# Pooled attention ahead of a gated feed-forward product on one core: a new order of ScalarE's and VectorE's work inside the slots

## The chip, the cores and the metric

One core of one Trainium2 chip runs the whole kernel in one launch. The metric is the device time in microseconds of one execution; of several executions the median counts.

## What is computed

The reference, cut to what matters (B = 8 batches, H = 8 heads, S = 576 rows, D = 64, all float32; 4608 tokens, model width 512, inner width 1024):

```
k_p = k.reshape(B, H, 72, 8, D).mean(axis=3)          # pooling: 72 keys a head
v_p = v.reshape(B, H, 72, 8, D).mean(axis=3)
scores = (q @ k_p.T) / sqrt(D); scores -= scores.max(-1)
attn = exp(scores); attn /= attn.sum(-1) + 1e-9
x = (attn @ v_p)  ->  4608 tokens x 512               # heads side by side
out = ((x @ w1) * (x @ w2)) @ w3 @ w_out
```

The kernel multiplies w3 and w_out once into W (1024 x 512), so the last line becomes `out = ((x @ w1) * (x @ w2)) @ W`.

## The kernel before

**Exact products from two parts.** A float32 operand is written as a hi part (rounded by ScalarE's copy into another number type) and a lo part (source minus hi, on VectorE or GpSimd), and a product is three passes on TensorE: hi-hi, hi-lo, lo-hi. So each operand that TensorE is to use needs first an instruction of ScalarE, then a subtraction that waits for it: `split` (L152 hi, L153 lo), the lo parts of W_out (L177) and of w3 in the first slots (L194), R (L451 hi, L453 lo), the probabilities PT (L486 hi, L487 lo), x (L510 hi, L511 lo), g (L546 hi, L551 lo). The weights arrive in a packed form, each value as two words: `high` (L135, ScalarE) unpacks the one word, `low` (L140, VectorE) the other, and `conv_b` (L148, VectorE; "the combine") joins them. Only `low` has read the second word of the raw cell, so a later load into that cell waits for it.

**Chunks and tiles.** The 4608 tokens go in 12 chunks of 384. A chunk has 3 token tiles of 128 where it lies in one batch, and 4 of 96 where two batches meet in it (chunks 1, 4, 7, 10). Per tile the attention goes: scores of heads 0 to 3 and of heads 4 to 7 on TensorE (L404, `s_mm`, two "passes"); `soft1` for each pass: the extreme of the scores (L420, VectorE) and exp. Five tiles (chunk 0's three and two of chunk 1) have their exps on ScalarE alone, four a pass, each with its sum read out by the accumulator (L430); the others subtract on VectorE (L422), take exp on ScalarE (L425) and sum on VectorE (L426). Then `soft2` on VectorE (L439 and L441 on the sums, L442 scales all 8 heads' exps), `soft3` (R, the 8 keys of each head that don't fit the 128-wide layout, as hi on ScalarE and lo on VectorE), transposes of the probabilities (L464) and of R (L474) on TensorE, `pt_post` (PT hi and lo), and per head pair attention times v (L499 to L502) and x's hi and lo (`av_post`). In the main loop, per chunk and block j of the inner width, `a_mm` and `b_mm` (L525), `a_post` (copy, L535), `b_post` (product g, L545, and its hi), `g_lo` (L551) and `out_mm` (L560).

**What sets the order.** The program is written out by a plan: `at(kind, k, fn)` notes a step, and the steps are emitted sorted by slot (the integer part of k), then by kind in the order L (loads), P (vector and scalar work), M (main matmuls), A (attention matmuls), then by the fraction of k, then by when they were noted. Each engine runs its own instructions in the order of emission, so a step that emits for ScalarE and VectorE puts an instruction into each queue, and a waiting instruction holds up all behind it on that engine. A fraction of k matters only among steps of one kind in one slot. Slot numbers: F0 = 4 is the first slot of the product of w3 and W_out, which takes two slots for each of 16 steps; K0 = 20 is its middle, where the attention of chunk 0 begins to be prepared; M0 = 36 is the first slot of the main loop, 24 slots a chunk. `w_block` (L164) is the vector and scalar work of one weight step in the first slots: new weights (unpack), the weights of the step before (hi and w3's transpose with its lo) and W_out's lo part of two steps before. From step 8 on `w_conv`, `w_conv2` and `w_split` (L209 to L219) do the same for w3 alone. w1 and w2 are unpacked by `w12_conv`, `w12_conv2` and `w12_split` (L221 to L237) in slots M0-6 to M0+17; their lo part is on GpSimd but for three. `plan_att` (L604) places the attention of a chunk, one chunk ahead of the main loop's use; in chunk 1 a tile begins every 3 slots from M0+3. Beside it stand the pooling sums of k (`prep_k`; three of them on VectorE, L319, the others on GpSimd), the 32 x 32 transposes of q on VectorE (`tr_q`, L276), and v's remainder, the 8 keys of v that belong to R (`prep_vr`, L380: sums on GpSimd, then a copy and two scalings on ScalarE, L381 to L384; `prep_vr2`, L392: four additions on GpSimd).

**Buffers.** Scores, transposes and x share three PSUM buffers ("att", L65), so TensorE's next attention step also waits until one of the three has been read.

Of the kernel before, what the change touches and what calls it, by code (L numbers as in the profile page):

```python
# [18 lines left out]
def kernel(  # L19
# [143 lines left out]

    def w_block(v):  # L164


# [587 lines left out]
```

## Time and profile before

| | us |
|---|---|
| median of 3 runs | 807.65 (805.84 to 809.54) |
| the profiled execution | 805.16 |
| its span | 803.4 |
| TensorE busy | 777.9 (97%) |
| VectorE busy | 431.7 (54%) |
| ScalarE busy | 288.0 (36%) |
| GpSimd busy | 196.1 (24%) |
| mean granted TensorE clock | 0.989 |

The span is the time from the first to the last recorded instruction of the profiled execution; its own time has 1.8 us around that. PE is TensorE (PEld its weight loads), DVE VectorE, ACT ScalarE, POOL GpSimd, SP the queue that issues the loads. A busy share is an average over the span; an idle engine's bracket in a timeline says how long it stood still ahead of an instruction and which instruction ended that.

### The profile page before, as it was taken

The page shows a single profiled execution, that of the slowest core. Times are in us where ns is not written, and L with a number is a line of the kernel's source. Part 1 is how long each engine was busy: PE and PEld are TensorE (multiplying, and loading weights), DVE is VectorE, ACT ScalarE, POOL GpSimd, SP SyncE. Part 2 cuts the span into 40 slices and gives each one's busy share as a digit, 9 for nine tenths or more (in the row PEclk, how much of TensorE's full clock was granted, in tenths as well). Part 3 has the DMA queues.
Part 4 walks back from the last instruction along what each step waited for, and adds up shares of the span by engine and source line. Part 5 has one row for each costly group of instructions (what it writes and reads, how often), then busy time and mean ns, then how long its engine had stood idle before and what let it go on. Part 6 is the DMA issues. An engine that isn't in the chain of part 4 may idle for free.

```text
span 803.4 us, 11625 instructions
## 1 busy us (share of the span) xinstructions
PE 777.9 (97%) x4344; PEld 722.2 (90%) x4344; DVE 431.7 (54%) x873; ACT 288.0 (36%) x727; POOL 196.1 (24%) x234
## 2 busy tenths in 40 slices
PE   7899888999999999999999999999999999999998
PEld 6677777899999999999999999999999999999997
DVE  6968989465373375374374374474454455452112
ACT  5567565332243233242242333232242332332211
POOL 2155465107007302025008102034028020000000
PEclk8999999999999999999999999999999999999999
DMA  9988960045034030062043030071143110100101
GB/s 333 267 206 217 273 145 1 1 94 123 1 72 120 27 80 1 1 143 75 1 95 109 27 67 1 17 157 44 43 85 91 53 26 1 40 1 1 40 1 39
DMA packets 106632, 62.63 MB, mean 78 GB/s; under 512 B 73680, under 2 KB 90320, under 8 KB 106576
## 3 DMA queue, kind: packets, MB, share of 16 engines
q1 hardware_dynamic: 106576, 61.89, 30.1%
q8 instruction: 34, 0.56, 0.3%
q14 instruction: 22, 0.18, 0.1%
HBM read 52.43 MB, written 9.44 MB: 77 GB/s over the span
## 4 chain that ended last, share of the span: by engine, by line
PE 85%; DVE 7%; DMA 4%; issue 2%; ACT 2%; SPq 0%; DVEq 0%
PE o L560 24%; PE a L525 24%; PE b L525 23%; PE att L404 4%; PE o L586 2%; DMA st<-in_k_dram 2%; PE att L464 2%; DVE wb L140 1%; DVE wb L148 1%; PE att L501 1%; PE att L500 1%; PE att L502 1%; PE att L499 1%; PE att L474 1%; DMA raw<-in_moe_w_out_dram 1%
## 5 line engine op out<-in xcount | busy, mean ns | idle before, releaser
L525 PE MATMUL a<-xT,hl 128*128 128x384 f32 x1152 | 223.1, 342 | 0.0
L525 PE MATMUL b<-xT,hl 128*128 128x384 f32 x1152 | 220.3, 339 | 0.4 <-DVE Wc L153 0.4
L525 PEld LDWEIGHTS a<-xT,hl 128*128 128x128 f32 x1152 | 205.0, 190 | 4.9 <-POOL hl L153 0.2
L525 PEld LDWEIGHTS b<-xT,hl 128*128 128x128 f32 x1152 | 198.7, 188 | 0.8 <-DVE Wc L153 0.8
L560 PE MATMUL o<-Wc,gh 128*128 128x512 f32 x576 | 183.6, 400 | 0.0
L560 PEld LDWEIGHTS o<-Wc,gh 128*128 128x128 f32 x576 | 105.1, 189 | 17.3
L545 DVE TENSOR_TENSOR a<-b,a 128x384 f32<-128x384 f32 x96 | 53.1, 553 | 123.5 <-PE b L525 123.5
L362 POOL TENSOR_TENSOR st<-st 72x512 f32<-72x512 f32 (+1 forms) x53 | 73.0, 1377 | 173.2 <-DMA st<-in_k_dram 161.0
L560 PE MATMUL o<-Wc,gl 128*128 128x512 f32 x288 | 114.0, 396 | 0.0
L535 ACT COPY a<-a 128x384 f32<-128x384 f32 x96 | 46.1, 480 | 179.9 <-PE a L525 160.6
L546 ACT CAST gh<-a 128x384 fp32r<-128x384 f32 x96 | 49.2, 512 | 148.4 <-DVE a L545 148.4
L551 DVE TENSOR_TENSOR gl<-a,gh 128x384 fp32r<-128x384 f32 x96 | 59.4, 619 | 35.8 <-ACT gh L546 35.4
L375 POOL TENSOR_TENSOR vbd<-vm,vbd 64x256 fp32r<-64x256 f32 x16 | 13.3, 833 | 249.8 <-ACT vbd L374 248.2
L560 PEld LDWEIGHTS o<-Wc,gl 128*128 128x128 f32 x288 | 54.1, 188 | 12.5
L511 DVE TENSOR_TENSOR xT<-att,xT 128x384 fp32r<-128x384 f32 x48 | 26.5, 556 | 70.0 <-ACT xT L510 70.0
L426 DVE TENSOR_REDUCE sm<-E 128x4 f32<-128x288 f32 (+1 forms) x70 | 31.6, 451 | 46.3 <-ACT E L425 46.3
L404 PE MATMUL att<-kbd,qT 128*128 128x144 f32 (+1 forms) x320 | 52.1, 286 | 0.2 <-ACT E L430 0.2
L420 DVE TENSOR_REDUCE mx<-att 128x4 f32<-128x288 f32 (+1 forms) x80 | 36.0, 450 | 28.8 <-PE att L404 28.7
L425 ACT ACTIVATE E<-E 128x288 f32<-128x288 f32 (+1 forms) x70 | 31.1, 445 | 55.4 <-DVE E L422 55.4
L404 PEld LDWEIGHTS att<-kbd,qT 128*128 128x128 f32 (+1 forms) x320 | 46.6, 179 | 1.1 <-ACT E L430 0.5
L586 PE MATMUL o<-hl 128*128 128x512 f32 x144 | 42.3, 430 | 3.3 <-DVE hl L177 3.3
L363 POOL TENSOR_TENSOR st<-st 72x256 f32<-72x256 f32 (+1 forms) x53 | 41.8, 789 | 4.2
(87 smaller groups left out, 806.4 us busy)
## 6 DMA issues: line engine op xcount, KB each, us to landing
raw<-in_moe_w_dram SPq DMA_DIRECT2D x32, 512.0 KB
st<-in_k_dram SPq DMA_DIRECT2D x32, 288.0 KB
out_dram<-ob SPq DMA_DIRECT2D x35, 256.0 KB
st<-in_v_dram SPq DMA_DIRECT2D x32, 256.0 KB
qs<-in_q_dram SPq DMA_DIRECT2D x128, 48.0 KB
raw<-in_moe_w_out_dram SPq DMA_DIRECT2D x8, 512.0 KB
st<-in_v_dram SPq DMA_DIRECT2D x64, 64.0 KB
qs<-in_q_dram SPq DMA_DIRECT2D x96, 24.0 KB
```

The source lines that it names most:

```text
L362: nc.gpsimd.tensor_tensor(out=t[:, :, 0:4], in0=t[:, :, 0:4], in1=t[:, :, 4:8], op=ALU.add)
L363: nc.gpsimd.tensor_tensor(out=t[:, :, 0:2], in0=t[:, :, 0:2], in1=t[:, :, 2:4], op=ALU.add)
L404: nc.tensor.matmul(out=ps[:nt, 2 * KP * j:2 * KP * (j + 1)], lhsT=qT[n][:, pr, off:off + nt], rhs=kbd[b % 2][:, pr], start=True, stop=True,)
L420: nc.vector.tensor_reduce(out=mx[:nt, hs], in_=sv, axis=AX.X, op=ALU.min)
L426: nc.vector.reduce_sum(out=sm[:nt, hs], in_=E[:nt, hs], axis=AX.X)
L525: nc.tensor.matmul(out=o, lhsT=w12[j, w][sw][:, kt * P:(kt + 1) * P], rhs=x[sx][:, kt], start=(i == 0), stop=(i == 3 * NK - 1))
L535: nc.scalar.copy(out=a, in_=gt[m, j][:, :CH])
L545: nc.vector.tensor_tensor(out=g, in0=ps[:, :CH], in1=g, op=ALU.mult)
L546: nc.scalar.copy(out=gh, in_=g)
L551: nc.vector.tensor_tensor(out=gl, in0=g, in1=f(gh), op=ALU.subtract)
L560: nc.tensor.matmul(out=oacc[m][t], lhsT=(gh, gl)[sg][:, c], rhs=W[j][sw], start=(j == 0 and i == 0), stop=(j == NJ - 1 and i == 2))
L586: nc.tensor.matmul(out=wacc[h][it], lhsT=w3t[s][sa][:, it * P:(it + 1) * P], rhs=wo[j][sb], start=(j == 0 and i == 0), stop=(j == NJ - 1 a ...
```

## The change

Each pair of a hi and a lo part is taken apart: `late` emits the hi part at once and notes the lo part, and a step `lo` of its own emits it, further back in the slot by its fraction. In the first slots `w_high` emits the two unpacks of ScalarE ahead of the rest (0.2 slots ahead, so in the slot before), and `w_block` has another order on VectorE. The sums of the exps (L426) go from `soft1` to `soft2`, as one sum over all 8 heads, and `soft2`, `soft3` and the new `soft4` (R's lo part) are placed three slots behind the slot of the tile's second pass, at fractions 0.1, 0.3 and 0.8 (`soft2` came two slots behind it, `soft3` with R's lo part three). v's remainder is cut in two: `prep_vr1`, the part on ScalarE, comes at 1.3 slots behind `prep_vr`, and `prep_vr2` a slot later than before. g's hi part leaves `b_post` and goes to 2.35, its lo part to 2.9. x's and PT's lo parts go to fractions 0.5 and 0.55.

```diff
+    def sub(out, a, b, eng=nc.vector):
+        eng.tensor_tensor(out=out, in0=a, in1=b, op=ALU.subtract)
...
+    los = {}
+    def late(key, src, hi, lo, eng=nc.vector):
+        nc.scalar.copy(out=hi, in_=src)
+        los[key] = lo, src, f(hi), eng
+    def lo(*key):
+        sub(*los.pop(key))
...
+    def w_high(v):
+        w_tiles(v)
+        high(raw["w3", v], stage["w3", v][1])
+        high(raw["wo", v], stage["wo", v][1])
+
     def w_block(v):
         new, mid, old = v < NJ, 0 <= v - 1 < NJ, 0 <= v - 2 < NJ
+        if mid:
+            w3t[v - 1] = hl_cell(4 + (v - 1) % 4)
+            late(("w3t", v - 1), w_turn(v - 1), *w3t[v - 1])
+            wo[v - 1] = hl_cell(8 + v - 1)
+            late(("wo", v - 1), f(stage["wo", v - 1][0]), *wo[v - 1])
+        if old:
+            lo("wo", v - 2)
         if new:
-            w_tiles(v)
...
-            high(raw["w3", v], z3)
-            low(raw.pop(("w3", v)), r3)
-            high(raw["wo", v], zo)
-        if old:
-            s = v - 2
-            nc.vector.tensor_tensor(out=wo[s][1], in0=f(stage["wo", s][0]), in1=f(wo[s][0]), op=ALU.subtract)
+            low(raw.pop(("w3", v)), stage["w3", v][0])
+            conv_b(*stage["w3", v])
+        if mid:
+            lo("w3t", v - 1)
         if new:
-            if v > 0:
-                low(raw["wo", v], ro)
-            conv_b(r3, z3)
-        if mid:
-            ps = w_turn(v - 1)
-            w3t[v - 1] = hl_cell(4 + (v - 1) % 4)
-            nc.scalar.copy(out=w3t[v - 1][0], in_=ps)
...
-            conv_b(ro, zo)
-        if mid:
-            wo[v - 1] = hl_cell(8 + v - 1)
-            nc.scalar.copy(out=wo[v - 1][0], in_=f(stage["wo", v - 1][0]))
-        if mid:
-            nc.vector.tensor_tensor(out=w3t[v - 1][1], in0=ps, in1=f(w3t[v - 1][0]), op=ALU.subtract)
+            low(raw["wo", v], stage["wo", v][0])
+            conv_b(*stage["wo", v])
...
     def w_split(s):
-        split(ps, *w3t[s])
+        late(("w3t", s), w_turn(s), *w3t[s])
...
     def w12_split(j, w):
-        split(f(r), *w12[j, w], eng=nc.vector if (j, w) in LO_DVE else nc.gpsimd)
+        late(("w12", j, w), f(r), *w12[j, w], eng=nc.vector if (j, w) in LO_DVE else nc.gpsimd)
...
         pool_tree(stage.pop(("vr", b)), m)
+        stage["vrp", b] = hi, m
+
+    def prep_vr1(b):
+        hi, m = stage.pop(("vrp", b))
         nc.scalar.copy(out=hi, in_=m)
...
             nc.scalar.activation(out=E[:nt, hs], in_=E[:nt, hs], func=AF.Exp, scale=-1.0)
-            nc.vector.reduce_sum(out=sm[:nt, hs], in_=E[:nt, hs], axis=AX.X)
...
     def soft2(n, t):
         E, sm = Et[n, t], Mt.pop((n, t))[1]
+        if (n, t) not in SOFT_ACT:
+            nc.vector.reduce_sum(out=sm[:nt], in_=E[:nt], axis=AX.X)
...
     def soft3(n, t):
         for dup in range(2):
-            nc.scalar.copy(out=R[:nt, :, :, dup, 0], in_=er)
+            nc.scalar.copy(out=R[:nt, :, :, dup, 0], in_=rest_keys(n, t))
+
+    def soft4(n, t):
...
         for dup in range(2):
-            nc.vector.tensor_tensor(
-                out=R[:nt, :, :, dup, 1], in0=er, in1=f(R[:nt, :, :, dup, 0]), op=ALU.subtract)
+            sub(R[:, :, :, dup, 1], rest_keys(n, t), f(R[:, :, :, dup, 0]))
...
     def pt_post(n, t):
-        nc.scalar.copy(out=hi, in_=pv[:, :, :nt])
-        nc.vector.tensor_tensor(out=lo, in0=pv[:, :, :nt], in1=f(hi), op=ALU.subtract)
+        late(("pt", n, t), pv[:, :, :nt], hi, lo_)
...
     def av_post(n, pr):
-        nc.scalar.copy(out=xh, in_=ps)
-        nc.vector.tensor_tensor(out=xl, in0=ps, in1=f(xh), op=ALU.subtract)
+        late(("x", n, pr), ps, xh, xl)
...
     def b_post(m, j):
+        nc.vector.tensor_tensor(out=g, in0=ps[:, :CH], in1=g, op=ALU.mult)
+        gt[m, j] = g
+
+    def g_hi(m, j):
...
-        nc.vector.tensor_tensor(out=g, in0=ps[:, :CH], in1=g, op=ALU.mult)
-        nc.scalar.copy(out=gh, in_=g)
+        late(("g", m, j), g, gh, gl)
-    def g_lo(m, j):
-        nc.vector.tensor_tensor(out=gl, in0=g, in1=f(gh), op=ALU.subtract)
...
+    SL = 3
...
-            at("P", k + 2, soft2, n, t)
-            at("P", k + 3, soft3, n, t)
+            at("P", k // 1 + SL + 0.1, soft2, n, t)
+            at("P", k // 1 + SL + 0.3, soft3, n, t)
+            at("P", k // 1 + SL + 0.8, soft4, n, t)
             k = pt_at[t]
...
-            at("P", k + 1, pt_post, n, t)
-            at("P", k + 1, ptr_post, n, t)
+            at("P", k // 1 + 1, pt_post, n, t)
+            at("P", k // 1 + 1.05, ptr_post, n, t)
+            at("P", k // 1 + 1.55, lo, "pt", n, t)
...
-            at("P", av_at[pr] + 1, av_post, n, pr)
+            at("P", av_at[pr] // 1 + 1.1, av_post, n, pr)
+            at("P", av_at[pr] // 1 + 1.5, lo, "x", n, pr)
...
-        at("P", prep_r + 1, prep_vr2, b)
+        at("P", prep_r + 1.3, prep_vr1, b)
+        at("P", prep_r + 2.3, prep_vr2, b)
...
-        at("P", F0 + 2 * (s - 2), w_block, s)
+        if s < NJ:
+            at("P", F0 + 2 * (s - 2) - (0.2 if s else 0), w_high, s)
+        at("P", F0 + 2 * (s - 2) + 0.6, w_block, s)
...
-            at("P", k - 1.5, w_split, s)
+            at("P", k - 1.95, w_split, s)
+            at("P", k - 1.3, lo, "w3t", s)
...
             at("P", k + 4, w12_split, j, w)
+            at("P", k + 4 + (0.75 if (j, w) in LO_DVE else 0), lo, "w12", j, w)
...
-            at("P", k + 2.5, g_lo, m, j)
+            at("P", k + 2.35, g_hi, m, j)
+            at("P", k + 2.9, lo, "g", m, j)
```

In `plan_att` k is at this place the slot of the tile's second pass: s_at + 1 for chunks 1 to 11 and s_at + 0.5 for chunk 0.

## Rows read from the trace of the kernel before

**Rows 1.** The busy time by stretch. Columns: the stretch and its length in us, for each engine its busy time and (x instructions), the granted TensorE clock as a share of full speed, the busy share of the DMA engines, GB/s.
```profile
96.00:144.00 48.00, 39.02 (x205) 35.70 (x205) 43.81 (x72) 26.09 (x85) 28.24 (x24) 0.93 0.38 78
...
160.00:780.00 620.00, 620.00 (x3514) 584.60 (x3513) 299.97 (x654) 192.32 (x473) 131.22 (x162) 1.00 0.22 53
```

**Rows 2.** TensorE's waits ahead of 160 us: engine and line that waited, what ended the wait (engine, tile, line), us in all, how many, the longest.
```profile
PE att L474 <- ACT E L430: 4.7, 2, 3.9
PE o L586 <- DVE hl L177: 3.3, 3, 2.4
PE att L474 <- DVE R L453: 2.8, 2, 1.7
...
PE att L474 <- DVE E L422: 2.0, 1, 2.0
```

**Rows 3.** The timeline around 36 us. Columns: start, duration, engine, line, operation, written and read tiles, shape, count, and in brackets the idle time before it with what ended it.
```profile
35.21 1.89 DVE L319 TENSOR_REDUCE km<-st 72x128 f32<-72x1024 f32 x1 [0.26 <-DMA st<-in_k_dram]
...
37.02 0.67 DVE L177 TENSOR_TENSOR hl<-wt,hl 128x512 fp32r<-128x512 f32 x1
37.62 0.68 DVE L194 TENSOR_TENSOR hl<-att,hl 128x512 fp32r<-128x512 f32 x1
...
37.75 2.52 PE L586 MATMUL o<-hl 128*128 128x512 f32 x6 [2.35 <-DVE hl L177]
```

**Rows 4.** The timeline around 62 us, in the softmax of chunk 0.
```profile
61.05 0.76 DVE L442 TENSOR_TENSOR E<-E,sm 128x576 f32<-128x576 f32 x1
...
61.95 0.63 PE L464 MATMUL att<-ident,E 128*128 128x128 f32 x4 [0.20 <-DVE E L442]
...
63.61 0.44 PE L474 MATMUL att<-ident,R 128*128 128x128 f32 x2 [1.02 <-DVE R L453]
```

**Rows 5.** The timeline around 83 us, at x of chunk 0.
```profile
83.25 1.05 DVE L140 TENSOR_SCALAR wb<-raw 128x512 int32<-128x512 int32 x1
...
83.39 0.44 PE L499 MATMUL att<-PTh,vbd 128*128 128x384 f32 x1 [1.60 <-DVE xT L511]
```

**Rows 6.** The timeline of TensorE around 144 us: the last transposes of R of chunk 1.
```profile
143.97 0.36 PE L474 MATMUL att<-ident,R 96*128 96x96 f32 x2 [1.73 <-DVE R L453]
```

**Rows 7.** VectorE's waits from 92 us to 144 us.
```profile
DVE sm L426 <- ACT E L425: 2.0, 4, 0.5
DVE gl L551 <- ACT gh L546: 0.9, 1, 0.9
DVE wb L148 <- ACT wb L135: 0.8, 1, 0.8
```

**Rows 8.** VectorE's instructions from 96 us to 144 us, grouped by line: operation, written and read tiles, shape, x count, busy us in all, mean ns of one, idle time before them.
```profile
L148 DVE SCALAR_TENSOR_TENSOR wb<-wb 128x512 int32<-128x512 int32 x10 | 10.1, 1012 | 0.9 <-ACT wb L135 0.8
L140 DVE TENSOR_SCALAR wb<-raw 128x512 int32<-128x512 int32 x9 | 7.4, 822 | 0.0
L442 DVE TENSOR_TENSOR E<-E,sm 96x576 f32<-96x576 f32 x4 | 4.7, 1164 | 0.1
...
L426 DVE TENSOR_REDUCE sm<-E 96x4 f32<-96x288 f32 x4 | 1.8, 449 | 2.0 <-ACT E L425 2.0
...
L276 DVE STREAM_TRANSPOSE qT<-qs 128x384 f32<-128x384 f32 x2 | 1.1, 564 | 0.0
```

**Rows 9.** The same grouping of VectorE from 0 us to 160 us with different tiles kept apart, of it the two groups that belong to W_out.
```profile
L148 DVE SCALAR_TENSOR_TENSOR wt<-wt 128x512 int32<-128x512 int32 x8 | 5.5, 685 | 0.2 <-ACT wt L135 0.2
...
L140 DVE TENSOR_SCALAR wt<-raw 128x512 int32<-128x512 int32 x8 | 3.4, 420 | 0.9 <-DMA raw<-in_moe_w_out_dram 0.9
```

**Rows 10.** ScalarE's instructions from 96 us to 144 us, grouped by line.
```profile
L152 ACT CAST hl<-wb 128x512 fp32r<-128x512 f32 x12 | 7.3, 614 | 0.0
L135 ACT ACTIVATE wb<-raw 128x512 f32<-128x512 f32 x8 | 5.4, 674 | 0.0
...
L546 ACT CAST gh<-a 128x384 fp32r<-128x384 f32 x4 | 2.1, 516 | 1.0 <-DVE a L545 1.0
L425 ACT ACTIVATE E<-E 96x288 f32<-96x288 f32 x4 | 1.8, 444 | 8.5 <-DVE E L422 8.5
L451 ACT CAST R<-E 96x64 fp32r<-96x64 f32 x8 | 1.6, 246 | 5.9 <-DVE E L442 5.9
...
L383 ACT ACTIVATE vrh<-vrh,msk 128x128 f32<-128x128 f32 x1 | 0.4, 404 | 0.0
...
L381 ACT CAST vrh<-vrm 128x128 fp32r<-128x128 f32 x1 | 0.3, 282 | 0.0
```

**Rows 11.** The timeline around 113 us: a transpose of R in chunk 1, the matmuls behind it, and the first and last of four exps with their read-outs on ScalarE.
```profile
112.89 0.39 PE L474 MATMUL att<-ident,R 96*128 96x96 f32 x2 [3.86 <-ACT E L430]
...
113.06 3.89 PE L525 MATMUL a<-xT,hl 128*128 128x384 f32 x12
...
114.21 0.32 ACT L430 ACTIVATE E<-att,mx 96x72 f32<-96x72 f32 x1
...
115.31 0.21 ACT L430 ACTIVATION_READ_ACCUMULATOR E<-att,mx 96x1 f32 x1
```

**Rows 12.** The timeline around 294 us, in the main loop.
```profile
291.32 2.27 PE L525 MATMUL a<-xT,hl 128*128 128x384 f32 x12
...
294.51 0.56 DVE L487 TENSOR_TENSOR PTl<-att,PTh 128x384 fp32r<-128x384 f32 x1 [1.41 <-ACT PTh L486]
...
296.50 0.65 PE L404 MATMUL att<-kbd,qT 128*96 128x144 f32 x4
```

More of the change, by code (lines that the diff above doesn't have):

```diff
@@ L149, in conv_b @@
             out=r, in0=z.bitcast(I32), scalar=3, in1=r, op0=ALU.logical_shift_left, op1=ALU.bitwise_or)
+    def sub(out, a, b, eng=nc.vector):
+        eng.tensor_tensor(out=out, in0=a, in1=b, op=ALU.subtract)
     def split(src, hi, lo, eng=nc.vector):
         nc.scalar.copy(out=hi, in_=src)
-        eng.tensor_tensor(out=lo, in0=src, in1=f(hi), op=ALU.subtract)
+        sub(lo, src, f(hi), eng)
+    los = {}
[4 more added lines that the diff above has]
+        sub(*los.pop(key))
     def w_tiles(s):
@@ L162, in w_tiles @@
         stage["w3", s] = W_cell(0, 4 + s % 4, I32), W_cell(1, 4 + s % 4, F32)
+    def w_high(v):
+        w_tiles(v)
+        high(raw["w3", v], stage["w3", v][1])
+        high(raw["wo", v], stage["wo", v][1])
     def w_block(v):
         new, mid, old = v < NJ, 0 <= v - 1 < NJ, 0 <= v - 2 < NJ
-        if new:
-            w_tiles(v)
-            r3, z3 = stage["w3", v]
-            ro, zo = stage["wo", v]
-            high(raw["w3", v], z3)
-            low(raw.pop(("w3", v)), r3)
-            high(raw["wo", v], zo)
-        if old:
-            s = v - 2
-            nc.vector.tensor_tensor(out=wo[s][1], in0=f(stage["wo", s][0]), in1=f(wo[s][0]), op=ALU.subtract)
-        if new:
-            if v > 0:
-                low(raw["wo", v], ro)
-            conv_b(r3, z3)
-        if mid:
-            ps = w_turn(v - 1)
-            w3t[v - 1] = hl_cell(4 + (v - 1) % 4)
-            nc.scalar.copy(out=w3t[v - 1][0], in_=ps)
-        if new:
-            if v == 0:
-                low(raw["wo", v], ro)
-            conv_b(ro, zo)
-        if mid:
-            wo[v - 1] = hl_cell(8 + v - 1)
-            nc.scalar.copy(out=wo[v - 1][0], in_=f(stage["wo", v - 1][0]))
-        if mid:
-            nc.vector.tensor_tensor(out=w3t[v - 1][1], in0=ps, in1=f(w3t[v - 1][0]), op=ALU.subtract)
+        if mid:
[5 more added lines that the diff above has]
+            lo("wo", v - 2)
+        if new:
+            low(raw.pop(("w3", v)), stage["w3", v][0])
+            conv_b(*stage["w3", v])
+        if mid:
+            lo("w3t", v - 1)
+        if new:
+            low(raw["wo", v], stage["wo", v][0])
+            conv_b(*stage["wo", v])
     def warm(n):
@@ L443, in soft2, with rest_keys @@
             out=E[:nt], in0=E[:nt], in1=sm[:nt].unsqueeze(2).broadcast_to([nt, H, KP]), op=ALU.mult)
+    def rest_keys(n, t):
+        nt = tok_tiles(n)[t][2]
+        return Et[n, t][:nt].rearrange("p (a h) (x e) -> p a (h x) e", h=2, e=KR)[:, :, 0:18:17, :]
     def soft3(n, t):
-        b, off, nt = tok_tiles(n)[t]
-        E = Et[n, t]
+        nt = tok_tiles(n)[t][2]
         R = Rt[n, t] = p2.tile([P, NPR, 2, 2, 2, KR], F32R, tag="R", name="R")
-        er = E[:nt].rearrange("p (a h) (x e) -> p a (h x) e", h=2, e=KR)[:, :, 0:18:17, :]
         for dup in range(2):
-            nc.scalar.copy(out=R[:nt, :, :, dup, 0], in_=er)
+            nc.scalar.copy(out=R[:nt, :, :, dup, 0], in_=rest_keys(n, t))
+    def soft4(n, t):
+        nt = tok_tiles(n)[t][2]
+        R = Rt[n, t][:nt]
         for dup in range(2):
-            nc.vector.tensor_tensor(
-                out=R[:nt, :, :, dup, 1], in0=er, in1=f(R[:nt, :, :, dup, 0]), op=ALU.subtract)
+            sub(R[:, :, :, dup, 1], rest_keys(n, t), f(R[:, :, :, dup, 0]))
     Tp = {}
@@ L484, in pt_post @@
         pv = Tp.pop((n, t))
-        hi, lo = PTh[n][:, :, off:off + nt], PTl[n][:, :, off:off + nt]
-        nc.scalar.copy(out=hi, in_=pv[:, :, :nt])
-        nc.vector.tensor_tensor(out=lo, in0=pv[:, :, :nt], in1=f(hi), op=ALU.subtract)
+        hi, lo_ = PTh[n][:, :, off:off + nt], PTl[n][:, :, off:off + nt]
+        late(("pt", n, t), pv[:, :, :nt], hi, lo_)
     def ptr_post(n, t):
@@ L542, in b_post @@
         g, ps = gt[m, j]
+        nc.vector.tensor_tensor(out=g, in0=ps[:, :CH], in1=g, op=ALU.mult)
+        gt[m, j] = g
+    def g_hi(m, j):
+        g = gt[m, j]
         gh = p2.tile([P, CH], F32R, tag="gh", name="gh")
         gl = p2.tile([P, CH], F32R, tag="gl", name="gl")
-        nc.vector.tensor_tensor(out=g, in0=ps[:, :CH], in1=g, op=ALU.mult)
-        nc.scalar.copy(out=gh, in_=g)
+        late(("g", m, j), g, gh, gl)
         gt[m, j] = (g, gh, gl)
-    def g_lo(m, j):
-        g, gh, gl = gt[m, j]
-        nc.vector.tensor_tensor(out=gl, in0=g, in1=f(gh), op=ALU.subtract)
     def out_mm(m, j):
```

1 line of the change is left out of this document (removed).

## The prediction

> **What bounds the kernel now.** I read the busy time by stretch first [rows 1]. From 160 us to 780 us TensorE is busy all of 620.00 us and no wait of it is listed there; VectorE is busy 299.97 of them, about half. In that part a new order on ScalarE or VectorE can only cost, and it costs only if something becomes so late that TensorE waits. All there is to gain lies ahead of 160 us, and TensorE's waits there [rows 2] tell where: 3.3 us on the weights' lo parts (L177), and 9.5 us at L474, the transposes of R, the remainder columns of the attention. From 96 us to 144 us VectorE is the bound: busy 43.81 of 48 us [rows 1], and TensorE waits for what it gives. So the reader has to ask of each moved instruction where in VectorE's queue it lands, and what TensorE needs behind it.
>
> **The change, part by part.** In "slot M0+7" and the like, M0 and K0 are those of the kernel; slot M0 is reached at about 87 us.
>
> Weights, slots up to K0. ScalarE's queue keeps its order here, since w_high only moves the two hi conversions ahead of a slot in which they were first anyway. On VectorE, W_out's lo part comes first in its slot and the second `low` last. The loads on SP wait for the same `low`, up to one 0.68 us subtraction later, and the transfers that they feed already queue; nothing there. What TensorE waits for L177 ahead of 35 us now (3.3 less 2.4, at most 0.9 us [rows 2]) may go, but is lost again at the next point: the pooling sum of k (L319) starts when its load lands, at 35.21 us, holds VectorE 1.89 us, and TensorE waits 2.35 us for the W_out lo part behind it [rows 3]. In the new order w_conv2(9), a combine (L148), stands ahead of that lo part: it starts one combine later, **+0.6 us** (the pitch from 37.02 to 37.62 us; the row's duration is 0.68). TensorE is nearly gapless from there to 56 us, so it keeps that loss. Bounds: 0 and +0.7.
>
> Softmax of chunk 0, slot K0+6. soft2 moves here from the slot before, both tiles ahead of the remainder's lo part. The first transpose (L464) waited 0.20 us and the second (L474) 1.02 us, for R's lo part [rows 4]. The scaling of tile 0 would be ready at nearly the same time as now, because the combine ahead of it waits for ScalarE in either order; R's lo part now has the scaling of tile 1 and one w3 lo part ahead of it, less what was ahead before: **+0.4 us**, between 0 and +1.2 (one whole soft2, whose scaling alone takes 0.76 us [rows 4]).
>
> x of chunk 0, slot M0-1. A `low` moves ahead of the first x lo part, for which TensorE waits 1.60 us [rows 5]: **+0.35 us**, between 0 and the 1.05 us that this `low` took there. The w12 lo part that moves back a slot is used by b_mm some 4 us later.
>
> Chunk 1, slots M0+3 to M0+17, VectorE-bound. Here waits and work of VectorE count one for one, since the last R transpose of the chunk (143.97 us now [rows 6]) waits for VectorE's last instruction ahead of it.
> - Gone: four waits of the sums for ScalarE's exp, 2.0 us, one of gl for gh, 0.9, one of a combine for its hi, 0.8 [rows 7]. **-3.7 us.** The sums become two reductions of 96x576 instead of four of 96x288 at 449 ns [rows 8]. No row has such a reduction of 96x576: not under 0.45 us and not over 0.90; I take 0.76, what the scaling takes for as many elements [rows 4]. **-0.3 us.**
> - New: the diff says hi first, but g_hi is put at 0.35 of its slot, and soft1, at 0, also emits ScalarE's exp, which waits for VectorE. So gh now stands behind exp, and gl, last on VectorE, stalls everything behind it. By durations of this very stretch [rows 9 to 11]: slot M0+5, exp 0.44, a hi conversion 0.67 and gh 0.52, less one `low` 0.42, 1.2 us; M0+8, four exps with their read-outs 1.3 us (114.21 to 115.52) and gh 0.52, less a combine 0.68, 1.1; M0+11, the same less a `low` as well, 0.6; M0+14, exp 0.44, a w12 hi 0.61, v's remainder on ScalarE 0.28 + 0.40 and a second scaling like it, gh 0.52, with nothing of VectorE's beside them, 2.6. At M0+16 R's lo part follows soft2 directly and waits for R's hi, two copies, 0.4. **+5.9 us**; bounds 0 (ScalarE so far ahead that nothing is waited for) and 8 (each wait longer by the one ScalarE instruction more that stands in its slot). I take the value worked out, since it is made of this stretch's own rows.
> - A transpose of q (L276) stands ahead of the last soft2: **+0.55 us** [rows 8].
> - Given back: in this stretch VectorE is stretched by GpSimd beside it: ten combines take 1012 ns [rows 8] against 685 [rows 9], nine `low` 822 against 420, four scalings 1164 against 760 [rows 4], and R's lo parts are longer too: 3.3 + 3.6 + 1.6 us and some 2 more, a quarter of the 43.81. Of 2.2 us more idle time a quarter would come back: **-0.6 us**, between 0 and -2.2.
>
> The sharing is also told by the Trainium skill, page "SBUF — State Buffer", section "Who interferes with whom": VectorE and GpSimd share a port pair as an exclusive lock, and the one that comes second is blocked for the other's whole instruction. By that rule alone, GpSimd would use VectorE's idle time in full, the give-back would be 2.2 us and the sum 1.6 us; the rows cannot tell a blocked instruction from a slow one, so I keep the quarter.
>
> Main loop, chunks 2 to 11: **0**. VectorE has half its time free. The R transposes come a slot after soft2, R's lo ends about 3.6 us after the scores that open the slot (two passes 0.9, soft2 1.9, R's hi and lo 0.8), TensorE arrives after some 4.9 us: a cover of 1.3 us, or two more in chunks of four tiles. If it went, the price would be what VectorE is late beyond it, in each of 33 tiles. v's remainder on GpSimd a slot later is used six or more slots on. The tail has only g's parts, in the old order on each engine.
>
> Sum: 0.6 + 0.4 + 0.35 - 3.7 - 0.3 + 5.9 + 0.55 - 0.6 = **+3.2 us** on the profiled execution's 805.16 us (803.4 us span and 1.8 around it), 808.4 us. That execution lies 2.5 us under the median of 807.65 us, so the median after should be **810.9 us**. About 0.5%, 4 us, can be told from no change here; the forecast is slower by less than that, "same".
>
> **Rivals.** *Faster.* ScalarE comes early enough that gl's new waits stay hidden in VectorE's backlog. For it: ScalarE is busy only about half of this stretch. Against it: its exps wait for VectorE itself. Then -3.7 - 0.3 + 0.55 + 1.35 = -2.1 us stays, and TensorE's waits at L474 shrink so far that its clock holds: after the 3.86 us wait the next twelve matmuls took 3.89 us [rows 11] at the lower granted clock (1.2 GHz), against 2.27 us at the higher (2.4 GHz) [rows 12], 1.6 us, and this happens twice in the stretch. -2.1 to -5.3, up to -6 with the 0.6 of the first part: 801.5 to 805.5, with 802.5 the likeliest. The Trainium skill, "TensorE: Matmul & The Clock Gate", section "HAM oscillation — how this bites in real kernels", has the same rule, that idle gaps throw the array back to half rate; this trace agrees with the 3.89 us just told. Chance 0.22, of which 0.04 stays within 0.5%.
>
> *Slower.* The same wait of gl, decided at the R transpose of chunk 1's first tile, slot M0+8: R's lo part now ends its slot on VectorE, behind soft2, a combine and a `low`, which stood behind it before. If it comes later than 114.5 us (112.89 now), VectorE's backlog never closes: no give-back (+0.6), and TensorE stays at the lower clock for one more group (+1.6) after each of one or two longer waits. 3.2 + 0.6 + 1.6 to 3.2 = +5.4 to +7: 813 to 814.7. For it: all of VectorE's new waits lie behind that point. Against it: TensorE then waits for VectorE anyway, and its own clock hardly counts. Chance 0.27.
>
> *Slower by the main loop.* In chunks 4, 7 and 10 the probabilities' lo part (L487) goes from first in its slot to behind soft2. Now it ends at 295.07 us, and TensorE takes the next score buffer at 296.50 [rows 12]. Behind two passes and soft2 it ends near 298.1: if that buffer is the one taken, 1.6 us at two places in three chunks, 9.6 us, 820. Against it: two other buffers of the three are free by then. Chance 0.08.
>
> **How the numbers follow.** Forecast 0.43 (within 0.5%), faster rival 0.22, slower ones 0.27 and 0.08. So faster by over 0.5% 0.18, within it 0.47, slower by over 0.5% 0.35. The range goes from the faster rival's end to a little over the slower one's, 801.5 to 815.5 us; what it leaves out is the main loop's rival and the tails, under 2 in 10. The forecast's own range is 807 to 812.
>
> **What would show it.** Right: TensorE gapless from 160 us on; its L177 wait near 38 us 0.6 us later; VectorE waits gl <- gh in the stretch to 146 us, over 4 us in sum and the longest near 2.6; no waits sm <- E; the last R transpose of chunk 1 some 3 us later than 143.97 us. Wrong: that transpose at 142 us or before, or any wait of TensorE's after 160 us.

## The result, and the profile after

The changed kernel takes 813.68 us (median of 6 runs, 810.76 to 814.23) against 806.95 us before (6 runs): a ratio of 1.0077, 95% interval 1.005 to 1.0103, slower by 0.8%. The profiled execution after took 813.76 us with a span of 812.0 us, 8.6 us more than the one before; the medians lie 6.7 us apart. The forecast was 810.9 us and "same", by which it meant within 0.5%; the measured time lies inside the stated range of 801.5 to 815.5 us, near its upper end, and outside the forecast's own range of 807 to 812.

Where the 8.6 us between the two profiled executions arose is read best by taking the same TensorE instruction in both traces. TensorE issues its 4344 matmuls and transposes in the same order in both kernels, so the difference of the two start times is the loss so far:

| start before, us | what TensorE is at | later after by, us |
|---|---|---|
| 13.1 | first weight step | 0.8 |
| 28.1 | sixth weight step | 2.5 |
| 54.9 | first scores of chunk 0 | 4.4 |
| 66.3 | behind R of chunk 0 | 6.7 |
| 80.6 | attention times v, chunk 0 | 7.0 |
| 87.0 | main loop begins | 10.5 |
| 108.5 | chunk 1, first transposes | 10.8 |
| 138.6 | chunk 1, ahead of its last tile | 5.2 |
| 146.1 | behind chunk 1 | 7.0 |
| 539.4 | main loop | 8.6 |

So three places ahead of the main loop lost about 4.4, 2.6 and 3.5 us, chunk 1 gained 3.8, and the main loop lost 1.6. The busy time by stretch of the kernel after (columns as in [rows 1]) shows the clock's part: it is 0.79 on the mean from 66 us to 74 us, behind R's wait, and 0.50, the lower of its two levels (1.2 GHz), from 92 us to 98 us, behind x's wait. Before, it was 1.00 in both stretches.

```profile
66.00:74.00 8.00, 5.31 (x25) 4.64 (x25) 5.80 (x13) 3.64 (x18) 2.43 (x3) 0.79 0.82 215
92.00:98.00 6.00, 6.00 (x19) 5.31 (x20) 2.90 (x6) 2.23 (x5) 0.00 (x0) 0.50 1.10 222
160.00:780.00 620.00, 618.77 (x3512) 583.05 (x3511) 304.75 (x622) 189.85 (x475) 132.79 (x162) 1.00 0.22 53
```

TensorE's waits ahead of 170 us after, beside [rows 2]: those for the weights' lo part doubled from 3.3 us, those at R's transposes went from 9.5 us to 6.3, the one for x from 1.6 us to 3.1, and transposes of the probabilities wait 2.1 us.

```profile
PE o L599 <- DVE hl L152: 6.8, 4, 2.7
PE att L489 <- DVE R L152: 6.3, 3, 2.7
```

The timeline after at the weights (beside [rows 3]) has the one combine that the prediction counted, at 40.61 us, between the pooling sum and W_out's lo part, and the wait of 2.35 us is 2.71. But where two waits of 0.53 and 0.46 us stood ahead of it before, three stand there now, of 1.37, 1.03 and 1.69 us. Ahead of the second, W_out's lo part starts behind a GpSimd addition and takes 1.76 us; the same instruction at 41.21 us takes 0.68.

```profile
28.66 1.36 POOL L367 TENSOR_TENSOR st<-st 72x512 f32<-72x512 f32 x1 [23.51 <-DMA st<-in_k_dram]
...
28.81 1.76 DVE L152 TENSOR_TENSOR hl<-wt,hl 128x512 fp32r<-128x512 f32 x1
...
30.62 2.11 PE L599 MATMUL o<-hl 128*128 128x512 f32 x8 [1.03 <-DVE hl L152]
...
35.77 2.11 PE L599 MATMUL o<-hl 128*128 128x512 f32 x8 [1.69 <-DVE hl L152]
...
40.61 0.68 DVE L148 SCALAR_TENSOR_TENSOR Wc<-Wc 128x512 int32<-128x512 int32 x1
...
41.95 2.62 PE L599 MATMUL o<-hl 128*128 128x512 f32 x8 [2.71 <-DVE hl L152]
```

The timeline after in the softmax of chunk 0 (beside [rows 4]): soft2 now follows a combine that waits 0.74 us for ScalarE, and a GpSimd addition starts in the middle of it. The scaling of 8 sums (L449) beside that addition takes 1.24 us; the same line takes 0.16 us for the other tile.

```profile
63.93 0.69 DVE L148 SCALAR_TENSOR_TENSOR Wc<-Wc 128x512 int32<-128x512 int32 x1 [0.74 <-ACT Wc L135]
...
65.30 1.56 POOL L367 TENSOR_TENSOR st<-st 128x512 f32<-128x512 f32 x1 [6.31 <-DMA raw<-in_moe_w_dram]
65.66 1.24 DVE L449 TENSOR_SCALAR sm<-sm 128x8 f32<-128x8 f32 x1
...
69.20 0.44 PE L489 MATMUL att<-ident,R 128*128 128x128 f32 x2 [2.69 <-DVE R L152]
```

At x of chunk 0 (beside [rows 5]) two things bring VectorE late to x's lo part, for which TensorE waits 3.07 us in place of 1.60. A combine ahead of the pooling sum, started beside GpSimd, takes 1.82 us, where the one in its place took 0.69 before; and the `low` that the change moved stands ahead of the lo part, which costs 0.33 us, from 90.94 to 91.27. Together that is 1.46 of the 1.47 us.

```profile
85.36 1.82 DVE L148 SCALAR_TENSOR_TENSOR wb<-wb 128x512 int32<-128x512 int32 x1
...
88.54 1.88 DVE L324 TENSOR_REDUCE km<-st 72x128 f32<-72x1024 f32 x1
...
90.94 0.42 DVE L140 TENSOR_SCALAR wb<-raw 128x512 int32<-128x512 int32 x1
91.27 1.48 DVE L152 TENSOR_TENSOR xT<-att,xT 128x384 fp32r<-128x384 f32 x3
...
91.88 0.69 PE L513 MATMUL att<-PTh,vbd 128*128 128x384 f32 x1 [3.07 <-DVE xT L152]
```

The combine in the kernel before:

```profile
78.22 0.69 DVE L148 SCALAR_TENSOR_TENSOR wb<-wb 128x512 int32<-128x512 int32 x1
```

VectorE's waits in chunk 1, 100 us to 153 us (beside [rows 7]): those of the sums and of the combine are gone, and gl waits for gh, as predicted, 4.1 us in sum with the longest 2.4.

```profile
DVE gl L152 <- ACT gh L162: 4.1, 4, 2.4
DVE R L152 <- ACT R L463: 1.0, 2, 0.7
```

VectorE's groups from 105 us to 150 us (beside [rows 8]): the merged sum takes 717 ns, and combines, scalings, R's lo part and the scalings of the sums are shorter.

```profile
L148 DVE SCALAR_TENSOR_TENSOR wb<-wb 128x512 int32<-128x512 int32 x10 | 8.0, 801 | 0.0
...
L452 DVE TENSOR_TENSOR E<-E,sm 96x576 f32<-96x576 f32 x4 | 4.4, 1099 | 0.1
...
L152 DVE TENSOR_TENSOR R<-E,R 96x64 fp32r<-96x64 f32 x8 | 2.8, 383 | 1.0 <-ACT R L463 1.0
...
L448 DVE TENSOR_REDUCE sm<-E 96x8 f32<-96x576 f32 x2 | 1.4, 717 | 0.0
L449 DVE TENSOR_SCALAR sm<-sm 96x8 f32<-96x8 f32 x4 | 1.4, 345 | 0.1
```

R's lo part and the scalings of the sums in the kernel before, from 96 us to 144 us:

```profile
L453 DVE TENSOR_TENSOR R<-E,R 96x64 fp32r<-96x64 f32 x8 | 3.9, 527 | 0.0
...
L439 DVE TENSOR_SCALAR sm<-sm 96x8 f32<-96x8 f32 x4 | 3.1, 776 | 0.0
```

In the main loop two R transposes of the profile wait, 0.74 and 0.49 us; this is the first:

```profile
196.35 1.27 POOL L367 TENSOR_TENSOR st<-st 72x512 f32<-72x512 f32 x1
...
196.44 1.40 DVE L152 TENSOR_TENSOR R<-E,R 128x64 fp32r<-128x64 f32 x2 [0.37 <-ACT R L463]
...
197.98 0.41 PE L489 MATMUL att<-ident,R 128*128 128x128 f32 x2 [0.74 <-DVE R L152]
```

### The profile page after: what moved, and what is told of

It is laid out like the page before. It is cut to its first block, busy times and chain, and to the rows that moved or that the text cites. A ratio compares the mean times of both kernels' runs of the same rounds, so it can differ in the third digit from the quotient of the medians.

```text
span 812.0 us, 11653 instructions
## 1 busy us (share of the span) xinstructions
PE 782.7 (96%) x4344; PEld 726.4 (89%) x4344; DVE 433.6 (53%) x838; ACT 284.6 (35%) x727; POOL 203.0 (25%) x234
## 4 chain that ended last, share of the span: by engine, by line
PE 83%; DVE 11%; ACT 3%; issue 2%; DMA 1%; SPq 0%; DVEq 0%; ACTq 0%
PE a L538 23%; PE o L573 22%; PE b L538 22%; PE att L413 4%; PE o L599 2%; PE att L479 2%; DVE hl L152 1%; DVE E L452 1%; PE att L515 1%; PE att L513 1%; PE att L514 1%; PE att L516 1%; ACT E L438 1%; DVE wb L148 1%; DMA raw<-in_moe_w_out_dram 1%
## 5 line engine op out<-in xcount | busy, mean ns | idle before, releaser
L367 POOL TENSOR_TENSOR st<-st 72x512 f32<-72x512 f32 (+1 forms) x53 | 75.6, 1426 | 169.8 <-DMA st<-in_k_dram 157.2
L152 DVE TENSOR_TENSOR gl<-a,gh 128x384 fp32r<-128x384 f32 x96 | 62.6, 652 | 71.1 <-ACT gh L162 70.8
L162 ACT CAST xT<-att 128x384 fp32r<-128x384 f32 x48 | 23.0, 479 | 64.6 <-PE att L516 64.6
```

The costliest lines, as they stand in the source:

```text
L152: eng.tensor_tensor(out=out, in0=a, in1=b, op=ALU.subtract)
L367: nc.gpsimd.tensor_tensor(out=t[:, :, 0:4], in0=t[:, :, 0:4], in1=t[:, :, 4:8], op=ALU.add)
```

## The experiments

Medians are of 6 to 12 runs. The kernel before took 806.47, 806.3 and 806.47 us beside the three groups; ratios are to it.

### One place undone in the changed kernel

**undo_weights**: the weights' steps in the old order.

```diff
-            at("P", F0 + 2 * (s - 2) - (0.2 if s else 0), w_high, s)
-        at("P", F0 + 2 * (s - 2) + 0.6, w_block, s)
+        at("P", F0 + 2 * (s - 2), w_block, s)     # old body
-            at("P", k - 1.95, w_split, s)
-            at("P", k - 1.3, lo, "w3t", s)
+            at("P", k - 1.5, w_split, s)          # hi and lo together
```

> The changed kernel with the old order of the weights' steps: w_block as before, no w_high, w3's hi and lo together. Theory A (each loss ahead of the main loop comes from the edit that stands at its place): TensorE's waits for W_out's lo part, 6.8 us in the changed kernel's profile and 3.3 before, fall back to 3 to 4, the 1.03 us at 30.6 us and the 1.69 us at 35.8 us go, and the median falls by 3 us, from about 813.7 to about 810.5. Theory B (the order itself costs only what the prediction summed, and the rest is which VectorE instruction happens to meet GpSimd's, which shifts with any edit): the median falls by 0.6 us or less, and the loss comes back further on, at R or at x of chunk 0.

Measured: 812.1 us, 1.0054 (1.0035 to 1.0074), 1.6 us under the changed kernel; the two intervals overlap, so this is not clear of noise. Its profile reaches chunk 0's scores only 0.1 us later than the kernel before, so the 4.4 us are gone, but then R's transposes wait longer than in the changed kernel, here for a score buffer that ScalarE's copy of PT's hi part frees. Behind it is the same place: soft2 after a combine that waits 1.61 us, and on ScalarE PT's hi part stands behind R's hi part, which waits for that soft2.

```profile
61.29 0.69 DVE L148 SCALAR_TENSOR_TENSOR Wc<-Wc 128x512 int32<-128x512 int32 x1 [1.61 <-ACT Wc L135]
...
67.68 0.66 PE L496 MATMUL att<-ident,R 128*128 128x128 f32 x2 [3.81 <-ACT PTh L162]
```

Both theories have a part: the place is right, and in this profile most of what it gives is lost again at R.

**undo_soft2_chunk0**: soft2 of chunk 0 a slot earlier.

```diff
-            at("P", k // 1 + SL + 0.1, soft2, n, t)
+            at("P", k + 2 if n == 0 else k // 1 + SL + 0.1, soft2, n, t)
```

> The changed kernel with soft2 of chunk 0 alone a slot earlier, where it was. Theory A: TensorE's wait for R's lo part near 69 us falls from 2.69 to about 1 us, and since it is then short the granted clock stays at its higher level from 66 to 74 us, so the median falls by 1.6 + 1.6, about 3 us, to 810.5. Theory B: 0.4 us or less, since the scalings are then stretched by GpSimd at another place.

Measured: 806.61 us, 0.9996 (0.998 to 1.0012): 7.1 us under the changed kernel, more than twice theory A's 3. This step undone, the kernel is back at the time before; the weights' loss and chunk 1's gain are still in it and nearly cancel. In its profile TensorE starts the main loop 3.6 us later than before instead of 10.5, since R's wait is 1.83 us, x's 1.98 us, and the lower clock from 66 to 74 us and from 92 to 98 us does not come.

**undo_x_chunk0**: x of chunk 0 at its old place.

```diff
-            at("P", av_at[pr] // 1 + 1.1, av_post, n, pr)
-            at("P", av_at[pr] // 1 + 1.5, lo, "x", n, pr)
+            at("P", av_at[pr] + 1 if n == 0 else av_at[pr] // 1 + 1.1, av_post, n, pr)
+            at("P", av_at[pr] + 1 if n == 0 else av_at[pr] // 1 + 1.5, lo, "x", n, pr)
```

> The changed kernel with x of chunk 0 (hi and lo, fractions of the slot) where it was, ahead of that slot's unpack. Theory A: TensorE's wait of 3.07 us near 92 us falls to about 1.6 and the lower granted clock from 92 to 98 us goes with it: 1.5 + 2.0, the median 3 us lower, 810.5. Theory B: only the 0.35 us of one unpack goes, the wait stays near 2.7 us, since VectorE comes late to this slot by the combine that GpSimd stretched ahead of it (1.82 us), and the median stays above 813.

Measured: 809.27 us, 1.0033 (1.0012 to 1.0054), 12 runs from 805.02 to 813.68. The wait for x is 1.73 us, as theory A had it. But in this profile R's wait is short too, which the edit cannot reach: the same addition of GpSimd comes here behind soft2, not inside it.

```profile
66.44 1.36 POOL L367 TENSOR_TENSOR st<-st 128x512 f32<-128x512 f32 x1 [7.11 <-DMA qs<-in_q_dram]
...
66.58 0.44 PE L489 MATMUL att<-ident,R 128*128 128x128 f32 x2 [1.26 <-DVE R L152]
```

So this median does not give the size of x's own share.

**undo_three**: the three diffs above together.

> The changed kernel with all three undone: the weights' order, soft2 of chunk 0 and x of chunk 0; chunk 1 and the main loop stay changed. Theory A: the three gains add up, 9 us, and the median is 804 to 805, below the kernel before by the 4 us that chunk 1 gained less the 1.7 us of the main loop. Theory B: 1.4 us or less, 812.

Measured: 803.75 us, 0.9957 (0.9936 to 0.9979): theory A, and faster than the kernel before. x's wait stays, however, at 2.79 us, with the old order of x, behind a stretched combine:

```profile
80.64 1.67 DVE L148 SCALAR_TENSOR_TENSOR wb<-wb 128x512 int32<-128x512 int32 x1
...
86.69 0.45 PE L520 MATMUL att<-PTh,vbd 128*128 128x384 f32 x1 [2.79 <-DVE xT L152]
```

### What chunk 1 gained from, and the main loop

**keep_chunk1**: the three undone, and soft2 a slot later in chunk 1 alone.

```diff
-            at("P", k // 1 + SL + 0.1, soft2, n, t)
+            at("P", k // 1 + SL + 0.1 if n == 1 else k + 2, soft2, n, t)
```

> The three undone, and soft2 of chunks 2 to 11 back in its old slot as well; chunk 1's soft2 and its merged sums, and all of g, PT, x and v's remainder stay changed. Theory A (in the main loop R's lo part comes late where GpSimd stretches soft2 or R beside it, because soft2 now stands in the same slot): TensorE's waits for R's lo part behind 160 us, 1.2 us in the changed kernel's profile, go to nothing, and the median is 1 to 2 us under the 803.75 of the kernel with the three undone. Theory B (the main loop's waits come from another edit, v's remainder or g's lo part): they stay, 803.75.

Measured: 801.17 us, 0.9941 (0.9913 to 0.9968). No wait of TensorE's is left behind 160 us, as theory A says; the median is 2.6 us under that of `undo_three`, though the two intervals overlap.

**keep_chunk1_old_sums**:

```diff
             nc.scalar.activation(out=E[:nt, hs], in_=E[:nt, hs], func=AF.Exp, scale=-1.0)
+            nc.vector.reduce_sum(out=sm[:nt, hs], in_=E[:nt, hs], axis=AX.X)
...
-        if (n, t) not in SOFT_ACT:
-            nc.vector.reduce_sum(out=sm[:nt], in_=E[:nt], axis=AX.X)
```

> The same with the sums of the exps back in soft1, one for each pass, right behind exp, in all tiles that have them. Theory A (chunk 1's gain is the sums' waits for exp): VectorE's waits sm <- E of 2.0 us come back in chunk 1 and the median rises by 2 us or a little more against keep_chunk1. Theory B (the gain is that soft2 stands a slot later, so that R's transposes find what they need): within 0.5 us of keep_chunk1.

Measured: 800.13 us, 0.9922 (0.9893 to 0.9951). VectorE's waits of the sums are back, and the median isn't higher: theory A falls. It does not show that such waits cost nothing, since gl's fell from 5.1 us to 2.7 at the same time, and the listed waits are 4.8 us in sum against 5.1.

```profile
DVE gl L152 <- ACT gh L162: 2.7, 4, 1.4
DVE sm L442 <- ACT E L441: 2.1, 4, 0.6
```

**keep_chunk1_old_soft2**:

```diff
-            at("P", k // 1 + SL + 0.1 if n == 1 else k + 2, soft2, n, t)
+            at("P", k + 2, soft2, n, t)
```

> keep_chunk1 with soft2 of chunk 1 a slot earlier too, so that soft2 stands everywhere in its old slot, with the sums merged in it. Theory A (the sums' waits are the gain): as keep_chunk1 or slower by the 0.5 us for which the merged sum then waits for exp in the same slots. Theory B (the later soft2 is the gain): slower than keep_chunk1 by 3 to 4 us, about the kernel before.

Measured: 804.15 us, 0.9978 (0.9957 to 0.9999), 3.0 us above `keep_chunk1`: theory B, though the two intervals just overlap. It is still some 2 us under the kernel before, at an interval that ends at 0.9999, so some of the gain may belong to edits that stay in it, which no run takes apart.

**keep_chunk1_g**:

```diff
-            at("P", k + 2.35, g_hi, m, j)
-            at("P", k + 2.9, lo, "g", m, j)
+            at("P", k + 2, g_hi, m, j)
+            at("P", k + 2.5, lo, "g", m, j)
```

> keep_chunk1 with g's hi part right behind the product, ahead of the next tile's exps on ScalarE, and g's lo part at its old fraction. Theory A (VectorE's waits gl <- gh in chunk 1, about 4 us, count one for one, as the prediction had it): they fall under 1.5 us and the median falls by 2.5 to 3 us, to about 799.5. Theory B (most of these waits are paid back, since VectorE's instructions beside GpSimd get shorter where it stands still less or more): the waits fall, the median by less than 1 us.

Measured: 800.87 us, 0.9927 (0.9901 to 0.9953). VectorE's waits and combines from 95 us to 147 us, first of `keep_chunk1`, then of this kernel:

```profile
DVE gl L152 <- ACT gh L162: 5.1, 5, 2.4
...
L148 DVE SCALAR_TENSOR_TENSOR wb<-wb 128x512 int32<-128x512 int32 x10 | 7.5, 754 | 0.0
```

```profile
DVE gl L152 <- ACT gh L162: 0.2, 1, 0.2
...
L148 DVE SCALAR_TENSOR_TENSOR wb<-wb 128x512 int32<-128x512 int32 x11 | 10.5, 959 | 0.2
```

4.9 us of gl's waiting are gone (1.4 us at PT's lo part are new), and the median falls by 0.3, within the noise: theory B. It names the reason too: scalings went from 1097 to 1268 ns and gl from 641 to 788, and over the same 71 instructions VectorE's idle time fell by 2.6 us while its busy time rose by 2.1.

### One part alone on the kernel before, and less work on GpSimd

**only_weights**: the weights' order alone.

```diff
-        at("P", F0 + 2 * (s - 2), w_block, s)
+        if s < NJ:
+            at("P", F0 + 2 * (s - 2) - (0.2 if s else 0), w_high, s)
+        at("P", F0 + 2 * (s - 2) + 0.6, w_block, s)     # new body
-            at("P", k - 1.5, w_split, s)
+            at("P", k - 1.95, w_split, s)
+            at("P", k - 1.3, lo, "w3t", s)
```

> The kernel before with nothing changed but the weights' order: w_high and the new w_block, and w3's hi and lo taken apart. Theory A (the new order costs what the changed kernel's profile shows from 28 to 42 us): TensorE's waits for W_out's lo part rise from 3.3 to 6 to 7 us, with new waits near 30 and 35 us, and the median rises by 2 to 3.5 us, to 808.5 to 810. Theory B (0.6 us, as predicted, or what undoing it gave, 1.6): 807 to 808.

Measured: 809.52 us, 1.0044 (1.002 to 1.0067), 3.0 us above: theory A. TensorE's waits for W_out's lo part ahead of 160 us:

```profile
PE o L590 <- DVE hl L165: 6.5, 4, 2.7
```

**only_soft2_chunk0**:

```diff
-            at("P", k + 2, soft2, n, t)
+            at("P", k // 1 + 3 if n == 0 else k + 2, soft2, n, t)
```

> The kernel before with soft2 of chunk 0 alone a slot later, behind one combine. Theory A (that place is what made R late in chunk 0): TensorE's wait for R near 64 us, 1.02 us before, grows to 2 to 3.5 us, the clock falls behind it, and the median rises by 2 to 4 us and in some executions by more. Theory B (it is late only together with the weights' new order): the median rises by 0.5 us or less.

Measured: 813.89 us, 1.0095 (1.0063 to 1.0127), 7.4 us above, more than theory A's 2 to 4. The combine that soft2 now follows waits 1.61 us for ScalarE, the probabilities make TensorE wait 1.36 us (0.20 in [rows 4]) and R 2.48 us (1.02), and x 3.45 us further on, although x's order is the old one here. GpSimd's addition starts only at 62.33 us, behind soft2, so at R the order alone makes it late:

```profile
58.83 0.69 DVE L148 SCALAR_TENSOR_TENSOR Wc<-Wc 128x512 int32<-128x512 int32 x1 [1.61 <-ACT Wc L135]
...
60.78 0.63 PE L464 MATMUL att<-ident,E 128*128 128x128 f32 x4 [1.36 <-DVE sm L439]
...
63.89 0.69 PE L474 MATMUL att<-ident,R 128*128 128x128 f32 x2 [2.48 <-DVE R L453]
...
88.55 0.44 PE L499 MATMUL att<-PTh,vbd 128*128 128x384 f32 x1 [3.45 <-DVE xT L511]
```

**only_soft2_chunk1**:

```diff
-            at("P", k + 2, soft2, n, t)
+            at("P", k + 2 + (n == 1), soft2, n, t)
```

> The kernel before with soft2 of chunk 1 alone a slot later, right ahead of R's parts; the sums stay in soft1, g stays as it was. Theory A (the later soft2 is the gain of chunk 1): the median falls by 3 us or more, to 803 or under, and TensorE's wait of 3.86 us at the first R of chunk 1 goes below 2. Theory B (the gain needs R's lo part set off from its hi part, or the other edits of chunk 1, as well): within 1.5 us of the kernel before, with R's lo part waiting for R's hi part in each tile.

Measured: 802.4 us, 0.9952 (0.993 to 0.9975), 4.1 us under the kernel before with one step moved. The first R of chunk 1 waits 2.44 us (3.86 in [rows 11]), not under 2, the two behind it 1.33 and 1.13 us, and the last R (1.73 in [rows 6]) has no wait any more:

```profile
111.71 0.39 PE L474 MATMUL att<-ident,R 96*128 96x96 f32 x2 [2.44 <-ACT E L430]
```

**less_gpsimd**: on the changed kernel.

```diff
     def pool_tree(t, dst):
-        nc.gpsimd.tensor_tensor(out=t[:, :, 0:4], in0=t[:, :, 0:4], in1=t[:, :, 4:8], op=ALU.add)
-        nc.gpsimd.tensor_tensor(out=t[:, :, 0:2], in0=t[:, :, 0:2], in1=t[:, :, 2:4], op=ALU.add)
         nc.gpsimd.tensor_tensor(out=dst, in0=t[:, :, 0], in1=t[:, :, 1], op=ALU.add)
```

> The changed kernel with the first two of the three additions of each pooling sum on GpSimd left out, 115 us of GpSimd's 203; so the pooled k and v are not the sums. Theory A (VectorE's instructions are stretched where GpSimd's meet them, and this made the late parts of the changed kernel later): in chunk 1 the unpacks' combines go from 801 ns to under 720 and the scalings from 1099 to under 900, TensorE's waits for R and for x ahead of 160 us, 9.4 us in sum, fall under 5, R's two waits in the main loop go, and the median falls by 5 us or more. Theory B (the order alone makes them late): 813, with the same waits.

Measured: 796.87 us, 0.9887 (0.9857 to 0.9918), 16.8 us under the changed kernel: theory A. x's wait is 0.33 us with the new order of x, R's in chunk 0 1.38 us, the second at the weights 0.18 us, and the main loop has none. TensorE's waits for R and x ahead of 160 us are 3.5 us in sum, where under 5 was expected. The scalings take 816 ns; the combines, at 821, miss the 720 expected (GpSimd's lo parts of w1 and w2 were left in). The kernel before was not run without these additions, so how much of the 16.8 us belongs to the change is open.

```profile
29.31 2.12 PE L597 MATMUL o<-hl 128*128 128x512 f32 x8 [0.18 <-DVE hl L152]
...
84.00 0.44 PE L511 MATMUL att<-PTh,vbd 128*128 128x384 f32 x1 [0.33 <-DVE xT L152]
```

## Why the prediction was right or wrong, point by point

The time came out at the rival "slower" (813 to 814.7 us), but by none of its mechanism: chunk 1, where that rival and the forecast had the loss, got faster. That the time lies in the range is luck, since the range spans the 14 us between rivals about chunk 1, and the loss arose ahead of it. The medians rose by 6.7 us, twice the forecast's +3.2, and its terms were wrong in place.

**Weights, +0.6: the term was mis-sized.** Alone it costs 3.0 us, five times as much and far over the bound of 0.7. At 38 us the mechanism was right, with +0.36 us (2.35 to 2.71) for 0.6. The rest lies ahead of it, where the prediction let 0.9 us of waits go. Two of the three waits there are the new order: ahead of the first (1.37 us at 13.87), W_out's lo part stands behind the whole unpack of the next block, and that behind w3's lo part, which waits 1.10 us for ScalarE; ahead of the third (1.69 us), it stands behind w3's unpack in the same slot. The second (1.03 us) is GpSimd's addition at 28.66 us beside the lo part; in `less_gpsimd` 0.18 us of it are left, and 5.3 of the 6.8 us in all.

**Softmax of chunk 0, +0.4: the step that failed.** The prediction said that the first scaling would be ready at nearly the same time, "because the combine ahead of it waits for ScalarE in either order". It does not stand ahead of it in the old order: there VectorE did both soft2 from 59.47 to 61.81 us and the combine after them, without a wait. In the new order it stands still for ScalarE first (0.74 us, 1.61 in `only_soft2_chunk0`) and does soft2 then. GpSimd can add to it: of R's 2.69 us in the changed kernel, 1.43 are two steps of soft2 made longer beside the addition (L449 1.24 us against 0.16, the scaling 1.11 against 0.76), and the other 1.26 us are what R still waits in `undo_x_chunk0`, where the addition comes behind soft2. The bound of +1.2 us was also too low, because it priced TensorE's wait alone; the clock fell behind the wait, and the lateness met GpSimd further on (x's wait is 3.07 us, and 1.98 with soft2 back). How late the order alone makes R differs between profiles, 0.24 us in `undo_x_chunk0` and 1.46 in `only_soft2_chunk0`; the medians agree. Moved alone, this step costs 7.4 us, and undoing it gives 7.1.

**x of chunk 0, +0.35: right for the order, wrong for the place.** The moved `low` costs 0.33 us, as worked out. The other 1.13 us of the wait are the combine of 1.82 us beside GpSimd, and slower matmuls behind the wait make up the other 2.0 us of the 3.5. The old order has the long wait too, in two of the kernels above (2.79 and 3.45 us), and in `less_gpsimd` the new one leaves 0.33 us. No term of the sum held that.

**Chunk 1, some +2 in sum (-3.7, -0.3, +5.9, +0.55, -0.6): the sign was wrong.** The waits were well foreseen: sums, gl and combine gone, gl now 4.1 us with 2.4 as the longest (2.6 forecast), the merged sum 0.717 us (0.76). In sum the waits went from 3.7 us to 5.1, by +1.4 where +2.2 was forecast. The term that failed is the give-back: the same 42 instructions of VectorE (ten combines, nine `low`, four scalings, eight lo parts of R, five of g, two of w1 and w2, four scalings of sums) take 34.6 us before and 28.3 after, 6.3 us less, where the prediction put 0.6 and at most 2.2. With that, VectorE's sum is near -5 us, and TensorE gained 3.8. `keep_chunk1_g` shows the same from the other side: waits taken away were paid back, by instructions that got longer.

What made them shorter is shown as far as the step goes: soft2 of chunk 1 a slot later, alone on the kernel before, gave 4.1 us. The prediction's sum has no term for it in chunk 1; its slower rival names the place and expects a loss. How the step does it stays open. In the kernel before, the first R's transposes waited 3.86 us for exps on ScalarE that read the scores [rows 11], and those exps for the next tile's extreme on VectorE, which stood behind soft2:

```profile
106.75 1.57 DVE L442 TENSOR_TENSOR E<-E,sm 96x576 f32<-96x576 f32 x1
...
111.05 0.44 DVE L420 TENSOR_REDUCE mx<-att 96x4 f32<-96x288 f32 x1
```

In `only_soft2_chunk1` soft2 still stands ahead of this extreme. What moved is a combine and a `low` that come ahead of soft2 there; this `low`, 1.48 us beside GpSimd before, takes 0.42, and the extreme comes 1.2 us earlier:

```profile
107.02 1.58 DVE L442 TENSOR_TENSOR E<-E,sm 96x576 f32<-96x576 f32 x1
...
109.87 0.44 DVE L420 TENSOR_REDUCE mx<-att 96x4 f32<-96x288 f32 x1
```

In the changed kernel the extreme comes ahead of soft2:

```profile
116.06 0.44 DVE L429 TENSOR_REDUCE mx<-att 96x4 f32<-96x288 f32 x1
...
117.63 1.51 DVE L452 TENSOR_TENSOR E<-E,sm 96x576 f32<-96x576 f32 x1
```

Whether the gain is score buffers read earlier, or instructions of VectorE that meet fewer of GpSimd's, no run separates. In the changed kernel R's transposes wait for R's lo part instead.

**Main loop, 0: nearly.** The cover of 1.3 us that the prediction named is real, but R's lo part beside GpSimd takes 1.40 us instead of some 0.44 before, and 0.74 us of TensorE's time goes at that tile. The prediction had named any wait of TensorE's after 160 us as a sign of being wrong, and two came, 1.2 us in sum. With soft2 back in its slot the waits go.

**The give-back, -0.6, measured -6.3.** The Trainium skill's rule, named in the prediction (page "SBUF — State Buffer", section "Who interferes with whom"), is that where VectorE and GpSimd want the port pair that they share, the second is blocked for the other's whole instruction. The trace agrees at 65.66 us: the scaling of 8 sums ends at 66.90 us, GpSimd's addition at 66.86. So it is neither a quarter given back nor a fixed share, but depends on which instruction meets which.

The rival of a faster kernel was half right: a gain in chunk 1 came, by another cause, and was lost ahead of chunk 1. Of the signs named, the gl waits and the missing waits of the sums came as forecast; the last R transpose of chunk 1 came 5.7 us later (149.69 us), not some 3, since 10.5 us had been lost ahead of the main loop.

## What to carry to other kernels

Before costing a moved step, write down what stands ahead of it on its engine in both orders, and take the wait that an instruction fills as a cost if the instruction leaves. In a stretch that looks bound by VectorE while GpSimd works beside it, do not take its waits alone as a cost or a gain: 4.9 us of them taken away came back, as another wait and as longer instructions. Look instead at which short step meets which of GpSimd's instructions, and at what TensorE waits for behind it. The same edit gained in chunk 1 and lost in chunk 0, so place such a step by chunk: `only_soft2_chunk1`, 802.4 us, `keep_chunk1`, `keep_chunk1_old_sums` and `keep_chunk1_g`, 800 to 801 us, beat both kernels.
